# The first loads of a fused attention and MLP kernel: two queues for the first operand, a later table load on ScalarE, and four idle products on TensorE

## The chip, the cores and the metric

The kernel runs on one core of one Trainium2 chip. The metric is the device time of one execution in microseconds (us), lower is better. Three runs of the kernel before gave 574.39, 576.44 and 576.57 us, so the median is 576.44.

The engines are TensorE (PE, and PEld for its weight loads), VectorE (DVE), ScalarE (ACT), GpSimd (POOL) and SyncE (SP). SP and ACT each issue transfers on a queue of their own; the profile calls the issuing side SPq and ACTq. All the transfers of the page's "q1" are SP's, and those of "q10" are ACT's.

## The reference

```python
# q, k, v, f_logit: (4, 8, 768, 48) float32
f = 1.0 / (1.0 + np.exp(-f_logit))
for t in range(S):
    state = f[:, :, t, :, None] * state + np.einsum('bhd,bhe->bhde', k[:, :, t], v[:, :, t])
    y[:, :, t] = np.einsum('bhd,bhde->bhe', q[:, :, t], state)
# y as rows: (3072, 384)
h = x @ w_in                                   # (384, 2048)
g = h * (1.0 / (1.0 + np.exp(-1.702 * h)))
out = g @ w_out                                # (2048, 384)
```

## The kernel before

**Units.** The sequence is cut into 12 units of 256 tokens (three for each of four batches). For each unit `attention(n)` makes the gated linear attention in six levels (`level`), each a set of small products (`score`, tile `sc`), a scaling of X by the gates (`promote`, L561) and a masked copy into `A` (`evacuate`). The MLP of earlier units fills TensorE between those steps. Up to unit 3 the order on all engines is written out by hand (`opening`, then `PLAN`); PE and POOL keep the program's order throughout.

**The opening.** Unit 0 needs its three operands first. `load_raw(n, j, engines)` brings f_logit (j = 0), q (j = 1) or k (j = 2) into `raw`: one transfer for each of four pairs of heads, pair `a` going to the queue `engines[a * len(engines) // NP]`. With one engine in the list all four are on one queue. f and k are issued by SP, q by ACT (six transfers, because the first token is shifted). Eight semaphores serve the hardware transfers in turn, so a ninth transfer waits for the landing of the one that had its semaphore before. In the opening that means: k's third transfer waits for f's second, k's fourth for f's fourth, q's third for f's first, q's fourth for f's third, q's fifth and sixth for q's first and second, and the two transfers of the first weights (`fetch_weights`, L221) for k's first and second.

**The turns.** `turn` (L390 to L404) transposes `raw` through TensorE: two pieces of eight products for each operand into PSUM tiles `t` (L395; each product leaves two records, so a piece is 16 records), and ScalarE takes each piece out by two activations (L400): Sigmoid into `F` for f, Copy into `X` for k and q. The order is f (`begin_f`), k (`begin_k`, which then copies `Kc`, L536), q (`begin`). Only then come the first `sc` products of level 0.

**What stands before them.** DVE clears `ones` and then the whole of `A` (L135). ScalarE runs one Sigmoid on `ones` (L134), whose only use is to have the function table loaded; DVE then writes the ones again (L136). `keep_up(2, 192, ...)` makes two products of `A`'s cleared columns on TensorE, whose result nobody reads.

```python
def keep_up(times, columns=(NL - 1) * 64, of=None):
    if times:
        pt = bank([P, columns], f"idle_{next(serial)}")
    for _ in range(times):
        lhs, rhs = of or (ident, masks.rearrange("p l f t -> p (l f t)"))
        nc.tensor.matmul(pt, lhsT=lhs, rhs=rhs, start=True, stop=True)
```

Of the kernel before, what the change touches and what calls it, by code (L numbers as in the profile page):

```python
# [12 lines left out]
AF = mybir.ActivationFunctionType  # L13
# [10 lines left out]
def kernel(  # L24
# [33 lines left out]
    nc = tc.nc  # L58
# [3 lines left out]
    P = 128  # L62
# [51 lines left out]
    A = const.tile([P, 2 * NP, 2, HS], F32, name="A")  # L114
# [3 lines left out]
    def bank(shape, name, lane=None):  # L118

        if lane is None:  # L120
            lane = chosen.pop(0) if chosen else next(turns) % 4
        return ps.tile(shape, F32, tag=f"mm{lane}", name=name, bufs=1)
# [8 lines that stand above are left out]

    ones = const.tile([P, 1], F32, name="ones")
    nc.vector.memset(ones, 1.0)
    nc.scalar.activation(ones, ones, AF.Sigmoid)  # L134
    nc.vector.memset(A, 0.0)  # L135
    nc.vector.memset(ones, 1.0)  # L136
    serial = count()
    flat_A = A.rearrange("p c f t -> p (c f t)")
    keep_up(2, 192, (flat_A[:, :P], flat_A[:, :192]))

    R = U // 32
    RW = R * D + HS - D
# [49 lines left out]
    for r in range(NGR):  # L192
        ffs = range(r * FG, (r + 1) * FG)
        for ff in ffs[::2]:
            f = slice(ff * P, (ff + 2) * P)
# [13 lines left out]
    def fetch_weights(engine=nc.sync):  # L209
        n = state["fetch"]  # L210
        assert n < len(pairs) and n - PAIRS_AHEAD < state["done"] // 2
        state["fetch"] += 1
        dst, parts = pairs[n]
        if moe_w_in.dtype == F32:
            for part, src in parts:
                nc.sync.dma_start(out=part(dst), in_=src)
            return
        bits = wp.tile([P, 2 * DM * 2], I32, tag="bits", name=f"bits_{n}", bufs=PAIRS_AHEAD)
        by_dst = bits.rearrange("p (c f) -> p c f", c=dst.shape[1])
        for part, src in parts:  # L220
            engine.dma_start(out=part(by_dst), in_=src.bitcast(I32))  # L221
        fetched[n] = by_dst.rearrange("p c (f two) -> p c f two", two=2)

    def begin_pair(m):
        if m not in fetched:
            assert moe_w_in.dtype == F32
            todo.append(None)
            return
        dst, bits = pairs[m][0], fetched.pop(m)
        ve, lo, hi = nc.vector, bits[..., 0], bits[..., 1]  # L230

        def tmp(tag, bufs):
            t = wp.tile([P, 2 * DM], F32, tag=tag, name=f"{tag}_{m}", bufs=bufs)
            return t.rearrange("p (c f) -> p c f", c=dst.shape[1])

        t = {}

        def high():  # L240
            t["s"] = tmp("s", 1).bitcast(I32)
            ve.tensor_scalar(t["s"], hi, 3, None, op0=ALU.logical_shift_left)

        def low():
            t["r"] = tmp("a", 2).bitcast(I32)
            if m in R_BY_ACT:
                nc.scalar.activation(t["r"], lo.bitcast(U32), AF.Copy, scale=2.0 ** -29)
            else:
                ve.tensor_scalar(t["r"], lo.bitcast(U32), 2.0 ** -29, None, op0=ALU.mult)

        def both():
            ve.tensor_tensor(dst.bitcast(I32), t["s"], t["r"], ALU.add)
        nc.scalar.activation(hi.bitcast(F32), hi.bitcast(F32), AF.Prelu, scale=2.0 ** -112, alpha=-(2.0 ** 32))
        if m in R_BY_ACT:
            low()
        else:
            todo.append(low)
        todo.extend((high, both, None))
# [7 lines left out]
    def convert():  # L266

        if len(todo) <= NOP // 2:
            begin_next()
        if todo and todo[0]:  # L270
            todo.pop(0)()
        if todo and todo[0] is None:
            todo.pop(0)
            state["done"] += 2
# [10 lines left out]
    def load_raw(n, j, engines=(nc.sync,)):  # L285
        if n >= NALL:
            return
        b, s0 = n // NU, n % NU * U
        src = (f_logit, q, k)[j]
        first = s0 - (j == 1)  # L290

        def span(head, token, dims, d=0):
            return bass.AP(src.tensor, src.offset + ((b * H + head) * S + token) * D + d, dims)
        if n < N_FILL or (n == N_FILL and j in BY_PE):
            for a in range(NP):
                engine = engines[a * len(engines) // NP]
                to = by_pair[j][32 * a:32 * (a + 1), :, :R * D]
                if first < 0 and a == 0:

                    for r, rows in ((1, 16), (17, 15)):  # L300
                        engine.dma_start(
                            out=to[r:r + rows], in_=span(0, r * R - 1, [[R * D, rows], [S * D, 2], [1, R * D]])
                        )
                    engine.dma_start(out=to[:1, :, D:], in_=span(0, 0, [[R * D, 1], [S * D, 2], [1, (R - 1) * D]]))
                else:
                    engine.dma_start(out=to, in_=span(2 * a, first, [[R * D, 32], [S * D, 2], [1, R * D]]))
            return
        for f in (1, 0):
            for r in range(4):
                lo = 32 * (r % 2)  # L310
                width = R4 * D - lo
                part = span(r // 2, first + (0 if f else HALF), [[R4 * D, 32], [2 * S * D, NP], [1, width]], lo)
                nc.sync.dma_start(out=by_half[32 * r:32 * (r + 1), j, f, :, :width], in_=part)
            if f and first < 0:
                for r in range(4):
                    lo = 32 * (r % 2)
                    nc.sync.dma_start(
                        out=by_half[32 * r:32 * r + 1, j, f, :, :D - lo],
                        in_=q[b - 1, r // 2::2, S - 1:S, lo:].rearrange("a t d -> t a d"),
                    )  # L320
# [3 lines left out]
    def load_v(n):  # L324


        if n >= NALL:
            return
        b, s0 = n // NU, n % NU * U
        vts[n] = ld.tile([P, 2, DM], F32, tag="vt", name=f"vt_{n}", bufs=2)  # L330
        vrs[n] = ld.tile([P, DM], F32, tag="vr", name=f"vr_{n}", bufs=1)
        nc.sync.dma_start(
            out=vts[n][:, 1].rearrange("p (h d) -> p h d", h=H), in_=v[b, :, s0:s0 + HALF, :].rearrange("h p d -> p h d")
        )
        for i in range(4):
            t0 = s0 + U - 32 * (i + 1)
            nc.sync.dma_start(
                out=vrs[n][32 * i:32 * (i + 1)].rearrange("p (h d) -> p h d", h=H),
                in_=v[b, :, t0:t0 + 32, :].rearrange("h p d -> p h d"),
            )  # L340
# [1021 lines left out]
    def opening():  # L1362

        begin_f, begin, begin_k, begin_gates = units[0][0]
        next_f, next_q, next_k, next_gates = units[1][0]
        level, evacuate, turn_k = units[0][2]
        load_raw(0, 0)
        load_raw(0, 2)
        load_raw(0, 1, (nc.scalar,))
        fetch_weights()  # L1370
        begin_f()
        begin_gates()
        begin_k()
        begin()
        load_raw(1, 0)
        load_raw(1, 2)
        load_v(0)
        load_raw(1, 1)
        fetch_weights()
        fetch_weights()  # L1380
        for l in range(NL):
            chosen[:] = [2, 3][l % 2:][:1]
            level(l)
            if l in (2, 3):
                next_f((0, 4)[l - 2:][:1])
            elif l < NL - 1:
                keep_up(1)
            if l == 1:
                begin_pair(0)
                state["begin"] = 1  # L1390

        nc.scalar.activation(q_end, q_end, AF.Gelu_apprx_sigmoid)
        chosen[:] = [2, 3]
        turn_k(0)
        turn_k(2)
        for l in range(NL - 1):
            evacuate(l)
            if l == 1:
                units[0][3]()
        chosen[:] = [2, 3, 2, 3]  # L1400
        next_q()
        begin_pair(1)
        state["begin"] = 2
        evacuate(NL - 1)
        units[0][1][-2][1]()
        next_gates()
        for _ in range(NOP):
            convert()
        fetch_weights()

    fill = []
    opening()
    FIRST = 'k'
    PLAN = {
# [69 lines left out]
```

## Time and profile before

| | |
|---|---|
| median of three runs | 576.44 us (574.39 to 576.57) |
| the profiled execution | 574.38 us, of which the span is 572.6 |
| PE busy | 562.1 us (98% of the span) |
| DVE, ACT, POOL busy | 440.3, 291.7, 144.6 us |
| PE in the chain that ended last | 93% |
| first `t` product, first `sc` product | 4.63 us, 12.54 us |

The span runs from the first to the last instruction of the core; the 1.8 us beside it lie outside of it. The profile is of one execution, and its time is that of the quickest of the three runs. A busy PE is not a PE at its peak, and the shares of the whole span say little about the first 13 us, which are read here by themselves.

### The profile page before, as it was taken

The numbers are of one execution on the slowest core, as the hardware profiler recorded it, in microseconds if no ns is written. First come the engines' busy times: TensorE is split into PE (matmuls) and PEld (weight loads), VectorE is DVE, ScalarE is ACT, GpSimd is POOL, SyncE is SP. The second block draws the span as 40 slices with busy tenths as digits, with TensorE's granted clock in tenths as the row PEclk, the third lists the DMA queues.
The fourth block names the chain that finished last, engine by engine and source line by source line (L and its number), as shares of the span: only waits on it lengthen the run. The fifth ranks groups of instructions, "written<-read, shape, count | busy, mean of one in ns | idle before, by whom it ended". The sixth has DMA issues, their size and how long they took to land.

```text
span 572.6 us, 18599 instructions
## 1 busy us (share of the span) xinstructions
PE 562.1 (98%) x7870; PEld 515.3 (90%) x7870; DVE 440.3 (77%) x695; ACT 291.7 (51%) x592; POOL 144.6 (25%) x226
## 2 busy tenths in 40 slices
PE   7989999999999999999999999999999999999997
PEld 6767777686899999999999999999999999999996
DVE  2899688898997786887787888886888886462294
ACT  4755554332544573564564564564564573543440
POOL 4030320419451601501501501502501601303000
PEclk9999999999999999999999999999999999999999
DMA  7879695833262452363443344353361121001000
GB/s 194 194 181 230 152 254 135 238 81 87 72 177 58 125 134 57 99 158 79 114 123 68 99 118 104 108 129 69 98 158 44 50 55 30 30 2 29 29 1 28
DMA packets 85939, 60.01 MB, mean 105 GB/s; under 512 B 33441, under 2 KB 77633, under 8 KB 85857
## 3 DMA queue, kind: packets, MB, share of 16 engines
q1 hardware_dynamic: 85328, 58.21, 39.9%
q8 instruction: 62, 1.02, 0.8%
q10 hardware_dynamic: 529, 0.62, 0.4%
q14 instruction: 20, 0.16, 0.1%
HBM read 45.16 MB, written 8.91 MB: 94 GB/s over the span
## 4 chain that ended last, share of the span: by engine, by line
PE 93%; DVE 3%; DMA 1%; ACT 1%; issue 1%; SPq 0%; DVEq 0%
PE h L1080 28%; PE o_Y L938 14%; PE h L1174 10%; PE o_Z L938 9%; PE o L1188 7%; PE sc L467 6%; PE o_X L938 5%; PE o_W L938 4%; PE y L585 2%; PE y L743 2%; PE sc L696 2%; PE t L395 1%; DMA bits<-in_moe_w_in_dram 1%; DVE A L527 1%; DVE X L565 1%; DVE X L561 1%
## 5 line engine op out<-in xcount | busy, mean ns | idle before, releaser
L565 DVE TENSOR_TENSOR X<-X,tot 128x1024 f32<-128x1024 f32 x50 | 68.2, 1364 | 41.3 <-PE sc L467 37.0
L536 ACT COPY Kc<-X 128x512 f32<-128x512 f32 x72 | 48.4, 672 | 84.4 <-DVE X L565 71.2
L1080 PE MATMUL h<-E,w_in 128*128 128x128 f32 (+1 forms) x648 | 82.6, 276 | 0.0
L1080 PEld LDWEIGHTS h<-E,w_in 128*128 128x128 f32 x648 | 77.1, 192 | 0.5
L1108 DVE TENSOR_TENSOR g<-g,h 128x512 f32<-128x512 f32 (+1 forms) x92 | 55.4, 627 | 26.2 <-PE h L1080 18.9
L1038 POOL TENSOR_TENSOR E<-xT 128x128 f32<-128x128 f32 (+1 forms) x36 | 15.9, 453 | 231.3 <-DMA xT<-yT 231.3
L1174 PE MATMUL h<-xT,w_in 128*128 128x256 f32 x288 | 65.5, 382 | 0.0
L1174 PEld LDWEIGHTS h<-xT,w_in 128*128 128x128 f32 x288 | 53.9, 190 | 8.9 <-DMA xT<-yT 0.3
L1110 ACT ACTIVATE g<-g 128x512 f32<-128x512 f32 (+1 forms) x70 | 40.3, 588 | 34.9 <-DVE g L1108 34.8
L938 PE MATMUL o_Y<-T,S 128*128 128x192 f32 x320 | 57.6, 329 | 0.0
L938 PEld LDWEIGHTS o_Y<-T,S 128*128 128x128 f32 x320 | 52.3, 190 | 0.5
L1188 PE MATMUL o<-w_out,g 128*128 128x384 f32 x128 | 44.3, 492 | 0.0
L1099 ACT ACTIVATE g<-h 128x512 f32<-128x512 f32 (+1 forms) x70 | 37.0, 549 | 13.3 <-PE h L1080 11.4
L383 DVE STREAM_TRANSPOSE X<-raw 128x512 f32<-128x512 f32 x38 | 41.0, 1117 | 1.5 <-PE y L743 1.0
L527 DVE COPY_PREDICATED A<-masks,sc 128x256 f32<-128x256 uint32 (+1 forms) x98 | 42.0, 504 | 0.0
L758 ACT COPY yT<-y 48x256 f32<-48x256 f32 (+1 forms) x66 | 22.0, 369 | 30.1 <-PE y L743 29.6
L1080 PE MATMUL h<-E,N_c 128*128 128x128 f32 (+1 forms) x288 | 37.1, 275 | 0.0
L1188 PEld LDWEIGHTS o<-w_out,g 128*128 128x128 f32 x128 | 23.6, 190 | 14.6 <-issue 0.7
L1080 PEld LDWEIGHTS h<-E,N_c 128*128 128x128 f32 x288 | 35.1, 192 | 0.2 <-DVE osb L898 0.2
L467 PE MATMUL sc<-X,Kc 48*64 48x64 f32 x1344 | 28.2, 220 | 3.1 <-ACT Kc L536 1.4
L467 PEld LDWEIGHTS sc<-X,Kc 48*64 48x64 f32 x1344 | 24.0, 134 | 7.5 <-ACT Kc L536 3.6
L938 PE MATMUL o_X<-w_out,g 128*128 128x192 f32 x160 | 29.9, 332 | 0.3 <-ACT o_X L902 0.3
(131 smaller groups left out, 1088.2 us busy)
## 6 DMA issues: line engine op xcount, KB each, us to landing
bits<-in_moe_w_out_dram SPq DMA_DIRECT2D x8, 768.0 KB
raw<-in_f_logit_dram SPq DMA_DIRECT2D x48, 96.0 KB
raw<-in_k_dram SPq DMA_DIRECT2D x48, 96.0 KB
bits<-in_moe_w_in_dram SPq DMA_DIRECT2D x8, 576.0 KB
raw<-in_q_dram SPq DMA_DIRECT2D x44, 96.0 KB
k_tok<-z SPq DMA_DIRECT2D x64, 64.0 KB
kt<-k_tok SPq DMA_DIRECT2D x16, 256.0 KB
out_dram<-osb SPq DMA_DIRECT2D x20, 192.0 KB
```

The lines of the kernel that those rows point to most:

```text
L383: copied["turned"] = nc.vector.transpose(view(out, at, [[HALF, NP], [step, R4], [R4 * step, 32]]), by_half[:, j, f].rearrange("p a (j d) - ...
L467: nc.tensor.matmul(t["sc"][h][g * HS:(g + 1) * HS, a, s, :], lhsT=t["Kc", l][rows(h), x:x + HS], rhs=rhs(h, a, g), start=True, stop=True,)
L527: moved = nc.vector.copy_predicated(out=view(A, c * HALF + at, dims), mask=mask.bitcast(U32), data=got)
L536: nc.scalar.copy(c.rearrange("p (n two m) -> p n two m", two=2, m=m), view(X, KF * SLOT, [[2 * m, SLOT // (2 * m)], [(KR - KF) * SLOT + m, ...
L565: done = nc.vector.tensor_tensor(x, x, y, ALU.mult)
L938: nc.tensor.matmul(t[name], lhsT=lhs(f), rhs=rhs(f), start=(new and i == 0), stop=(i == HF - 1), skip_group_check=True,)
L1080: nc.tensor.matmul(ph[:, t], lhsT=WA[a][:, f // 2, f % 2 * P:(f % 2 + 1) * P], rhs=E[n][b], start=(root and t == 0), stop=not goes_on, ski ...
L1099: nc.scalar.activation(to, ph, AF.Copy, scale=float(sign))
L1108: copied["sum"] = nc.vector.tensor_tensor(to, to, part, ALU.add if sign > 0 else ALU.subtract)
L1110: nc.scalar.activation(to, to, AF.Gelu_apprx_sigmoid)
L1174: nc.tensor.matmul(ph, lhsT=w_in[:, ff // 2, c, ff % 2 * P:(ff % 2 + 1) * P], rhs=xTs[n][:, c, :], start=(c == 0), stop=(c == NK - 1))
L1188: nc.tensor.matmul(t["po"], lhsT=g[ff // FG][:, ff % FG, tt * P:(tt + 1) * P], rhs=w_out[:, ff, :], start=(ff == ffs[0]), stop=(ff == ffs[ ...
```

## The change

f's four transfers are split over SP and ACT, two on each. The Sigmoid that loads the table moves from the beginning of the program to behind ACT's eight transfers (two of f, six of q). The rewriting of `ones` moves from DVE to POOL. `A` is cleared in two pieces, the first of 192 columns, and `keep_up` makes four products of those 192 columns instead of two. The order of the instructions on each engine is otherwise that of before.

```diff
     ones = const.tile([P, 1], F32, name="ones")
     nc.vector.memset(ones, 1.0)
-    nc.scalar.activation(ones, ones, AF.Sigmoid)
-    nc.vector.memset(A, 0.0)
-    nc.vector.memset(ones, 1.0)
+    flat_A = A.rearrange("p c f t -> p (c f t)")
+    nc.vector.memset(flat_A[:, :192], 0.0)
+    nc.vector.memset(flat_A[:, 192:], 0.0)
     serial = count()
-    flat_A = A.rearrange("p c f t -> p (c f t)")
-    keep_up(2, 192, (flat_A[:, :P], flat_A[:, :192]))
+    keep_up(4, 192, (flat_A[:, :P], flat_A[:, :192]))
...
-        load_raw(0, 0)
+        load_raw(0, 0, (nc.sync, nc.scalar))
         load_raw(0, 2)
         load_raw(0, 1, (nc.scalar,))
+        nc.scalar.activation(ones, ones, AF.Sigmoid)
+        nc.gpsimd.memset(ones, 1.0)
         fetch_weights()
         begin_f()
         begin_gates()
```

## The prediction

> **What bounds the kernel now.** I read the page, then the waits of PE by stage, then the first 13 us: chain, timeline, windows. The page gives the shares of the chain that ended last:
>
> ```profile
> PE 93%; DVE 3%; DMA 1%; ACT 1%; issue 1%; SPq 0%; DVEq 0%
> ```
>
> PE's waits in the stretch from 60 to 160 us are 0.5 us in all, from 160 to 460 none are listed. All the change touches lies before 12.54 us, so the question is only how much sooner the first `sc` product starts, and whether that lead reaches the stretch in which PE never waits. The chain of the first 13 us:
>
> ```profile
> 0.74 0.40 SPq L306
> ...
> 2.12 2.38 DMA raw<-in_f_logit_dram
> 4.50 0.14 issue
> 4.63 5.18 PE t L395 x64
> 9.81 0.02 issue
> 9.84 0.67 ACT X L400 x2
> 10.50 0.02 issue
> 10.53 0.85 ACT Kc L536
> 11.38 1.11 ACT X L400 x4
> 12.49 0.04 issue
> ```
>
> f's last transfer is issued fourth on SP and lands at 4.50; then PE turns, then ScalarE. The timeline of ScalarE and its queue shows who else is near:
>
> ```profile
> 0.74 1.28 ACT L134 ACT_TABLE_LOAD   x1 [0.74 <-PEq L1468]
> 1.97 0.45 ACTq L301 DMA_DIRECT2D raw<-in_q_dram  x1
> 3.94 1.36 ACTq L306 DMA_DIRECT2D raw<-in_q_dram  x3
> 6.65 0.66 ACT L400 ACTIVATE F<-t 128x256 f32<-128x256 f32 x2 [4.41 <-DMA raw<-in_q_dram]
> 8.09 0.66 ACT L400 ACTIVATE F<-t 128x256 f32<-128x256 f32 x2 [0.78 <-PE t L395]
> 8.96 0.66 ACT L400 ACTIVATE X<-t 128x256 f32<-128x256 f32 x2 [0.21 <-PE t L395]
> 9.84 0.66 ACT L400 ACTIVATE X<-t 128x256 f32<-128x256 f32 x2 [0.21 <-PE t L395]
> ```
>
> ScalarE waits for PE 0.78 + 0.21 + 0.21 = 1.20 us between the first F and Kc: PE is late, by its own pace. The windows of L395 alone show why:
>
> ```profile
> 5.60:6.60 1.00, 1.00 (x13) 1.00 (x11) 1.00 1.07 299
> 6.60:7.60 1.00, 1.00 (x13) 1.00 (x11) 1.00 0.68 156
> 7.60:8.60 1.00, 1.00 (x22) 1.00 (x20) 1.00 0.92 317
> ```
>
> The first count is of records that touch the window: 13 in a us until 7.6, 22 behind it. The single records start in pairs 0.213 us apart before, 0.109 behind: the array runs at half pace up to 7.65 us, although the clock column reads 1.00 in all three rows (the trace's first clock record is a 1.0 at 7.65; nothing is recorded before). A piece of 16 records costs 1.71 us slow and 0.87 fast.
>
> **The change part by part.** All in the profiled execution's time (574.38 us, its span 572.6 and 1.8 around it).
>
> *A in two pieces, four idle products.* The clearing of A costs 0.91 us for 1024 columns, `ones` 0.06 for one; 192 columns lie near 0.06 + 0.16 = 0.22 us. It starts at 1.05 as before, so PE starts at 1.33 instead of 2.02. The four records of before start at 2.02, 2.50, 2.82 and 3.14; eight would start from 1.33 to 3.73 and leave PE free for the turns at 4.05. The other 832 columns end near 2.0 as now, and DVE's next job waits for POOL anyway (0.31 and 0.85 us idle). Cost of the split: nothing.
>
> *f on two queues.* The last of f's issues ends at 1.61 instead of 2.55. Landing: by issue time alone 4.50 - 0.94 = 3.56; if the bytes bound it, no sooner than 4.50. The four landed at 2.89, 3.38, 3.71 and 4.50 (the semaphores' counts in the trace), and 393 KB at the window's 235 GB/s (2.0 to 3.7 us) from the first packet at 1.8 is 3.5; I take 3.8. So the idle products, not f, set the start of the turns: 4.05 against 4.63, with 4.63 as the other end.
>
> *The half pace.* PE would be busy without a break from 1.33; now it stands still from 3.67 to 4.63. If the switch needs some 3 us of nearly full work (4.63 to 7.65 is 3.02), it comes between 4.3 and 7.65: each us sooner saves 0.49 us of the turns (1 - 0.109/0.213). The Trainium skill, "TensorE: Matmul & The Clock Gate", Part 1, says that the clock is released after a busy window of about 3.4 us and that this window runs freely, so the switch falls differently from run to run. This trace agrees in the 3.02 us of one execution; one trace cannot show the spread.
>
> *The table load.* This speaks against the change. ACT now issues two of f from 0.74, while q's first stays at 1.97 (it waits for POOL's clearing of raw, which ends at 1.94, not for the table). q's sixth waits for the landing of its second (4.97) and ends at 5.30. The load, 1.28, and the Sigmoid, 0.20, come behind that: the first F can start at 6.8, against 6.65 now. That PE has the piece earlier is of no use there. From then on, with PE ahead, ScalarE goes through without the 1.20 of waiting: four pairs at 0.69 (9.84 to 10.53), then 2.01 from Kc to `sc` (10.53 to 12.54) = 4.77, so `sc` starts at 11.57, 0.97 sooner. Bounds for the end of q's issues: 4.6 if its second lands with less beside it (F at 6.1, `sc` 1.67 sooner), or later (below). The skill's "ScalarE: Activation LUTs", What ACT_TABLE_LOAD costs, adds a drain of about 1.38 us to each switch. The row of the second load disagrees: Kc ends at 20.41, the load runs from 20.43 to 21.71 and its activation starts at 21.72. By that page `sc` would be at 12.95, 0.41 later than now.
>
> *k and q behind it.* Both are late already and only just hidden: k's fourth lands at 7.38 and is first read at 7.87; q's sixth lands at 9.17 and is read at 9.62. k's first still waits for POOL (1.97 against 2.59), its fourth for f's fourth (issued near 3.9 against 4.52): it lands near 6.8, no longer late. q's sixth is not sooner, and the first weights, which wait for k's first, start some 0.6 us earlier beside it. With q at 9.17, two pieces (1.76 and 0.2 to come out) end at 11.2, the last activations (0.6) at 11.85: `sc` at 11.9, 0.65 sooner. At 8.5 or less ScalarE decides (0.97); at 9.8 nothing is left. I take 0.75, from 0 to 1.67.
>
> *ones on POOL.* One small memset, 0.10 us by POOL's own, waiting for the Sigmoid (7.0). Behind it stands the first gate product, at 8.83 now, which needs all of F (near 8.2): hidden by a us; without that cover 0.1.
>
> *Behind 12.54.* Levels, conversions and later loads are released by these same engines. The second unit's f is turned at 16.45 and has landed at 13.57; the second weights' conversion at 25.24, landed at 22.99. These have 2 to 3 us to spare, so a lead of under 2 us passes through to PE's solid stretch and to the end.
>
> Sum: 574.38 - 0.75 = 573.6 for an execution like the profiled one. The median stands 2.06 above it. If those runs have the switch one window later (some 3.3 us), their turns cost 3.3 x 0.49 = 1.6 more, and the new kernel, with PE busy earlier, would mostly be spared it. I credit 0.65 of that 1.6: 576.44 - 0.75 - 0.65 = **575.0**, and 574.2 to 576.0 for this case alone.
>
> **The rivals.**
> 1. *q's last transfer takes it all.* The weights beside it push its landing to 9.8: 576.4. For: q's transfers need 2.4 to 3.9 us from issue to landing as weights join. Against: the dip of 156 GB/s from 6.6 to 7.6 leaves room.
> 2. *The clock decides.* The switch comes in all runs near 4.3, and the 2 us above the profiled run are the late switch: 574.38 - 1.2 = 573.2 as a median, 572.4 to 574.0. For: an idle gap of 0.96 us vanishes, and the three runs lie at two levels. Against: no run shows two switches, and ScalarE's F at 6.8 hides much of it.
> 3. *The table load takes the place of f's wait: slower.* ScalarE's chain needs 4.77 from the first F, so it loses from F at 7.77 on, which is q's issues ending at 6.27. If q's second needs as long as its sixth did (4.99 to 9.17, 4.18), it lands at 6.64, q's issues end at 6.96, F starts at 8.46, `sc` at 13.23: 0.69 late, 577.1. For: f's third and fourth now stand ahead of q on the queue. Against: f is 196 KB there and has landed by 3.8; q's second landed in 2.5 us beside the same bytes.
> 4. *The load costs more than its row.* Both loads of the trace let their activation follow within 0.02 us; the worst that a row bounds is a second load's time, 1.28 more: F at 8.1, `sc` at 12.87, 576.8. Against: both rows. The drain of the skill's page named above is a rule of this kind.
>
> That the change does not do what it says is excluded by the order of instructions: the ACT list has two f, six q, load, Sigmoid.
>
> **How the numbers follow.** Forecast 0.55; rival 1 0.12; rival 2 0.24; rival 3 0.06; rival 4 0.03. A measurement tells about 0.5% from no change, here 2.9 us, below 573.56 or above 579.3. Of rival 2 some 0.20 lies below 573.56, of the forecast 0.01; slower by so much needs F near 10.7 or a cause not seen here: 0.04. The range goes from rival 2's lower end to 576.9, two thirds of rival 3's price above the median: 572.4 to 576.9. It leaves out the costlier half of rival 3 and the tails of the others, under 2 in 10 together.
>
> **What would show it.** Idle records x8 from 1.33; `t` from 4.05; the load behind the last ACTq L306, F near 6.8; no wait for PE between the F and X pairs; `sc` near 11.8. Counts of 22 in L395's windows before 7.6 mean an earlier switch. Wrong: F after 7.8 (rival 3), PE waiting for q behind 9.2 (rival 1), or a lead at `sc` that is gone at 60 us.

## The result, and the profile after

The changed kernel has a median of 579.63 us (20 runs, 575.4 to 584.4) against 576.11 us of the kernel before on the same chip (20 runs, 574.4 to 577.4 but for a single one of 720.6): a ratio of 1.0053, 95% interval 1.0038 to 1.0068. The ratio leaves out the one execution in a slow state (584.4 us) and, like those below, is not the quotient of the two medians, which is 1.0061. The kernel is slower by half a percent; 575.0 us was predicted, with a range up to 576.9. The profiled execution took 575.4 us (span 573.7) and is one of the quickest: 6 of the 20 executions, with a mean granted clock of 0.999 or more, took 575.4 to 576.8 us, and the other 14, with 0.985 to 0.997, took 578.8 to 584.4. So two things have to be explained: about 1 us that the profiled executions show (575.40 against 574.38), and the rest of the 3.5 us between the medians, some 2.5 us, that they do not.

The page's line on the chain that ended last has 2% of DMA now, where there was 1%:

```profile
PE 92%; DMA 2%; DVE 2%; ACT 2%; issue 0%; ACTq 0%; POOL 0%; DVEq 0%; SPq 0%; POOLq 0%
```

The chain (start, duration, what) says which, as far as the turns of q:

```profile
2.38 3.53 DMA raw<-in_q_dram
5.90 0.02 issue
5.93 5.23 DMA raw<-in_q_dram
11.15 0.14 issue
11.29 1.98 PE t L394 x32
```

Before, the chain went from f's last transfer through 5.18 us of turns and through ScalarE. Now two transfers of q fill the time to 11.16: the second one (issued 2.38, landed 5.91), whose semaphore the sixth has to have, and the sixth itself, issued at 5.93 and landed at 11.16. Before, the sixth was issued at 4.99 and had landed at 9.17. f no longer stands in the chain. (Lines of the changed kernel have numbers one lower: L394 is L395 of before.)

The timeline of ScalarE, of SP and of PE shows the rest of the opening:

```profile
5.30 0.95 ACTq L305 DMA_DIRECT2D raw<-in_q_dram  x2
6.28 1.28 ACT L1369 ACT_TABLE_LOAD   x1 [6.28 <-DMA raw<-in_q_dram]
7.57 0.20 ACT L1369 ACTIVATE ones<-ones 128x1 f32<-128x1 f32 x1
7.68 0.64 ACT L399 ACTIVATE F<-t 128x256 f32<-128x256 f32 x2
8.51 0.66 ACT L399 ACTIVATE F<-t 128x256 f32<-128x256 f32 x2 [0.20 <-PE t L394]
```

```profile
5.53 0.87 SPq L220 DMA_DIRECT2D bits<-in_moe_w_in_dram  x2
```

SP's row of before, for comparison:

```profile
5.23 0.83 SPq L221 DMA_DIRECT2D bits<-in_moe_w_in_dram  x2
```

And PE, changed:

```profile
1.15 2.93 PE L130 MATMUL idle<-A 128*128 128x192 f32 x8 [1.15 <-DVE A L135]
4.79 6.24 PE L394 MATMUL t<-ident,raw 128*64 128x128 f32 x64 [0.71 <-DMA raw<-in_q_dram]
11.29 1.97 PE L394 MATMUL t<-ident,raw 128*64 128x128 f32 x32 [0.26 <-DMA raw<-in_q_dram]
14.00 0.70 PE L466 MATMUL sc<-X,Kc 48*64 48x64 f32 x32 [0.75 <-ACT X L399]
```

The eight records of the idle products end at 4.08, and the turns start at 4.79, not sooner than the 4.63 of before: the last of f's transfers lands at 4.55 from two queues, where it landed at 4.50 from one. SP's first weights, 768 KB in two transfers, start at 5.53 and so stand 0.40 us *ahead* of q's sixth; before they started at 5.23, 0.24 *behind* it. The first `sc` comes at 14.00 against 12.54. Of that 1.46 us, about 1.0 is left from 100 us on (each ScalarE instruction laid beside the same one of before), and 573.7 - 572.6 = 1.1 at the end.

The windows of L394 alone show the pace of the array (the first count is of records that touch the window; 22 in a us is full pace):

```profile
6.60:7.60 1.00, 1.00 (x13) 1.00 (x11) 1.00 0.60 110
7.60:8.60 1.00, 1.00 (x13) 1.00 (x12) 1.00 1.07 352
8.60:9.60 1.00, 1.00 (x14) 1.00 (x12) 1.00 1.06 249
9.60:10.60 1.00, 1.00 (x18) 1.00 (x16) 1.00 1.05 235
```

With four idle products in front the array stayed at half pace until 10.01 us, later than with two (7.65).

### The profile page after: what moved, and what is told of

Read it like the earlier page. It is cut to its first block, busy times and chain, and to the rows that moved or that the text cites. A ratio compares the mean times of both kernels' runs of the same rounds, so it can differ in the third digit from the quotient of the medians.

```text
span 573.7 us, 18608 instructions
## 1 busy us (share of the span) xinstructions
PE 564.4 (98%) x7874; PEld 517.5 (90%) x7874; DVE 439.3 (77%) x695; ACT 291.7 (51%) x592; POOL 145.3 (25%) x227
## 4 chain that ended last, share of the span: by engine, by line
PE 92%; DMA 2%; DVE 2%; ACT 2%; issue 0%; ACTq 0%; POOL 0%; DVEq 0%; SPq 0%; POOLq 0%
PE h L1079 28%; PE o_Y L937 14%; PE h L1173 10%; PE o_Z L937 9%; PE o L1187 7%; PE sc L466 6%; PE o_X L937 5%; PE o_W L937 4%; PE y L742 2%; PE y L584 2%; PE sc L695 2%; DMA raw<-in_q_dram 2%; DMA bits<-in_moe_w_in_dram 1%; DVE A L526 1%; PE t L394 1%; DVE X L564 1%
## 5 line engine op out<-in xcount | busy, mean ns | idle before, releaser
L1037 POOL TENSOR_TENSOR E<-xT 128x128 f32<-128x128 f32 (+1 forms) x36 | 17.1, 485 | 231.1 <-DMA xT<-yT 231.1
L409 POOL TENSOR_SCALAR F<-F 128x1024 f32<-128x1024 f32 x10 | 13.0, 1300 | 70.5 <-ACT F L412 70.5
L1177 ACT ACTIVATE g<-h 128x256 f32<-128x256 f32 x48 | 17.8, 382 | 24.7 <-PE h L1173 24.5
```

## The experiments

All ratios are to the kernel before on the same chip, with their 95% intervals. Times are of the profiled execution of each, in us. "q's sixth" is issued, landed, as the semaphores' counts in the trace have it; "weights" is the issue of the first of the first weights' two transfers; "switch" is when the array comes to full pace.

| run | first F | q's sixth | weights | first sc | switch | median us | ratio |
|---|---|---|---|---|---|---|---|
| before | 6.65 | 4.99, 9.17 | 5.23 | 12.54 | 7.65 | 576.11 | |
| changed | 7.68 | 5.93, 11.16 | 5.53 | 14.00 | 10.01 | 579.63 | 1.0053 [1.0038, 1.0068] |
| r1 changed again | 7.62 | 5.87, 10.70 | 5.60 | 13.55 | 6.42 | 579.06 | 1.0053 [1.0030, 1.0076] |
| r2 idle products only | 6.45 | 4.88, 7.87 | 5.31 | 12.41 | 6.04 | 576.02 | 1.0006 [0.9993, 1.0018] |
| r3 two queues only | 6.51 | 5.97, 12.46 | 5.37 | 15.30 | 9.93 | 578.31 | 1.0043 [1.0020, 1.0066] |
| r4 later table only | 6.93 | 5.17, 8.66 | 5.37 | 12.75 | 8.17 | 575.27 | 0.9992 [0.9980, 1.0003] |
| r5 changed, f on one queue | 6.89 | 5.14, 9.07 | 5.29 | 12.17 | 5.81 | 575.40 | 1.0000 [0.9988, 1.0012] |
| r6 changed, q's sixth on SP | 7.16 | 5.64, 7.97 | 6.17 | 11.50 | 4.16 | 575.30 | 0.9991 [0.9978, 1.0003] |
| r7 changed, more idle products | 7.74 | 5.93, 11.05 | 5.57 | 13.96 | 7.08 | 577.69 | 1.0047 [1.0022, 1.0072] |
| r8 idle products, q's sixth on SP | 6.93 | 5.27, 8.11 | 5.63 | 13.51 | 9.35 | 575.70 | 1.0002 [0.9991, 1.0013] |
| r9 before, q's sixth behind weights | 6.64 | 6.18, 12.51 | 5.32 | 15.36 | 10.30 | 579.52 | 1.0054 [1.0034, 1.0073] |
| r10 two queues, table first, q's sixth on SP | 5.63 | 5.46, 7.67 | 6.05 | 11.46 | 5.03 | 575.87 | 0.9998 [0.9982, 1.0015] |

**The parts one by one.** r1 is the changed kernel unaltered.

> The changed kernel once more, for the clock of its single executions. Two theories. Transfers: q's sixth transfer lands at 11.16 us instead of 9.17, the first sc product starts at 14.00 instead of 12.54, and this lead lost is all there is: every execution some 1 to 1.5 us longer (577 to 578), at a granted clock of 1.000. Clock: most executions lose one to five stretches of some 3.4 us at half clock (a mean of 0.997 for one, 0.994 for two), each worth about 1.7 us: median 579 to 580, and the executions at 1.000 lie near 576. If the profile falls on one of these, its clock rows show where.

It repeats the ratio, and 8 of its 12 executions have a mean granted clock below 0.998. r2 keeps the idle products and the split of `A`, with the table first and f on one queue:

```diff
 # before, with
-    nc.vector.memset(A, 0.0)
+    nc.vector.memset(flat_A[:, :192], 0.0)
+    nc.vector.memset(flat_A[:, 192:], 0.0)
...
-    keep_up(2, 192, (flat_A[:, :P], flat_A[:, :192]))
+    keep_up(4, 192, (flat_A[:, :P], flat_A[:, :192]))
```

> Only A in two pieces and four idle products instead of two; the table load first and f on SP alone as before. Transfers theory: q lands as before (9.2), PE is not sooner than f (4.6), so 575.5 to 576.2 and clock 1.000. Clock theory, by the idle products (PE released early, then too little work): means under 1.000 in most executions and a median of 578 to 580, as with the whole change.

r3 takes the two queues alone, r4 the later load alone:

```diff
 # r3: before, with
-        load_raw(0, 0)
+        load_raw(0, 0, (nc.sync, nc.scalar))
 # r4: before, with
-    nc.scalar.activation(ones, ones, AF.Sigmoid)
     nc.vector.memset(A, 0.0)
-    nc.vector.memset(ones, 1.0)
...
         load_raw(0, 1, (nc.scalar,))
+        nc.scalar.activation(ones, ones, AF.Sigmoid)
+        nc.gpsimd.memset(ones, 1.0)
```

> Only f on two queues; two idle products and the table load first as before. Transfers theory: q's second lands later, its sixth is issued behind the first weights and lands after 10.5, sc after 13.3: 576.8 to 577.8, clock 1.000. Clock theory, by the idle products: like before, 576.1. Clock theory, by PE standing still for q: means under 1.000 here too, median above 578.

> Only the table load behind q's transfers (and ones on POOL); f on SP alone, two idle products. Both theories: q's issues end at 5.3 as before, the first F starts at 6.8 instead of 6.65, sc at 12.6 to 12.7: 576.0 to 576.4 with a clock of 1.000. A drain or any hidden cost of the late load would show as F after 7.3.

r2 and r4 do nothing that can be measured; r3 carries the loss, 1.0043. Its q's sixth is issued behind both weights (5.37 and 5.73 against 5.97) and PE waits for it:

```profile
12.59 1.97 PE L395 MATMUL t<-ident,raw 128*64 128x128 f32 x32 [1.75 <-DMA raw<-in_q_dram]
```

r5 puts f back on one queue in the changed kernel and leaves the rest:

```diff
 # changed, with
-        load_raw(0, 0, (nc.sync, nc.scalar))
+        load_raw(0, 0)
```

> The changed kernel with f on SP alone again; the late table load and the four idle products stay. If the two queues are the cause: q's sixth lands near 9 as before, sc starts at 12.5 to 12.8, 575.3 to 576.3, and the granted clock is 0.999 or more in nearly all executions. If the late table load or the idle products were needed for the loss as well: 577 or more.

The loss is gone (1.0000). So the loss needs the two queues; the table and the idle products do not make it by themselves.

**Two queues, or the order behind them?** r6 leaves f on two queues and gives only q's sixth to SP, ahead of the weights:

```diff
 # changed, with
-        load_raw(0, 1, (nc.scalar,))
+        load_raw(0, 1, (nc.scalar, nc.scalar, nc.scalar, nc.sync))
```

> The changed kernel, f on two queues, with one transfer moved: q's sixth goes out on SP, where it stands ahead of the first weights. Theory that the weights overtake it: it lands by 9 instead of 11.16, PE does not wait for q, sc starts at 12.0 to 12.8, 575 to 576, the clock near 1.000. Rival, that two queues slow every landing (bytes shared with k and f): q's sixth lands after 10 here too, and the time stays above 577.5.

It lands at 7.97 though issued only 0.29 sooner, `sc` comes at 11.50 and the loss is gone (0.9991). r7 asks instead whether the pace of the array is to blame, by three idle products between the turns of k and of q:

```diff
 # changed, with
         begin_k()
+        chosen[:] = [1]
+        keep_up(3)
         begin()
```

> The changed kernel with three more idle products (320 columns, 1.6 us at full clock) between k's turns and q's, where PE now stands still for q. Theory that the clock falls back because PE has too little work there: the executions under 0.998 go from about 7 in 10 to a few, the median falls to 577 to 578, while sc stays at 13.5 to 14.2 in an execution at full clock. Rival, that the clock falls for another reason (later in the levels, or by the idle products in front): the share under 0.998 stays, and the median stays at 579 or above.

q lands as late as ever (11.05) and `sc` comes at 13.96. The outcome is mixed: the median falls to 577.69 and 5 of 12 executions are below 0.998, nearer to the first theory than to its rival, but the ratio of 1.0047 [1.0022, 1.0072] cannot be told from that of the change. Filling the wait does not undo the loss; whether it lessens it stays open. r8 joins r2 and the order of r6, r10 the two queues, the idle products and that order, with the table first as in the kernel before:

```diff
 # r8: r2, with; r10: changed, with the Sigmoid and the second memset of ones where they were before, and
-        load_raw(0, 1, (nc.scalar,))
+        load_raw(0, 1, (nc.scalar, nc.scalar, nc.scalar, nc.sync))
```

> The kernel before with the four idle products and with q's sixth transfer on SP ahead of the first weights; f on SP alone, table load first. If q's landing is what bounds the turns once the clock is released early, sc starts at 12.0 to 12.3 and the median is 574.6 to 575.3, a little under before. If k's landing (7.4 to 7.6) bounds: sc near 12.4, 575.3 to 575.8, no difference that shows.

> A version meant to beat both: f on two queues, four idle products, q's sixth on SP ahead of the first weights, and the table load first again. With q landing by 8 and F no longer behind the table (5.8 to 6.6 instead of 7.16), PE's own turns and k's landing (6.7) set the pace: sc at 11.2 to 11.6 where the clock is released early, median 574.6 to 575.4, at most 0.2% under before. If F was not what bounded: as with the late table load, 575.3.

Neither differs from the kernel before (1.0002, 0.9998), though r10 was meant to beat it and had `sc` 1.08 us sooner; where most of that lead goes, near 28 us, is seen below. r8's `sc` at 13.51 is an execution with a late switch (9.35), with q there at 8.11. r9 is the cleanest test: the kernel before, with f on one queue and the table first, and q's sixth on SP just behind the first weights.

```diff
 # before, with
-        load_raw(0, 1, (nc.scalar,))
         fetch_weights()
+        load_raw(0, 1, (nc.scalar, nc.scalar, nc.scalar, nc.sync))
```

> The kernel before (f on SP alone, table load first, two idle products) with one thing done alone: q's sixth transfer goes out on SP behind the two transfers of the first weights. If that order is the cause by itself: it lands at 11.5 or later, sc starts at 14.3 to 15.5, the median is 2 to 4 us over before (578 to 580), and a quarter or more of the executions have a clock under 0.998. If the loss needs f on two queues: no more than 0.5 us over before.

It has a loss as large as the change's, 1.0054, from the order alone. The order is a harsher one, behind both transfers of the weights, and `sc` is late by 2.82 us where the change had 1.46:

```profile
5.32 0.82 SPq L221 DMA_DIRECT2D bits<-in_moe_w_in_dram  x2
6.18 0.47 SPq L306 DMA_DIRECT2D raw<-in_q_dram  x1
```

```profile
12.64 1.97 PE L395 MATMUL t<-ident,raw 128*64 128x128 f32 x32 [1.54 <-DMA raw<-in_q_dram]
```

Issued 1.19 later than before, q's sixth lands 3.34 later. Sorted by its place against the first weights, the landings of q's sixth line up over all 20 profiled executions: issued 0.36 to 0.59 ahead (r2, r6, r8, r10, s4, t2) it lands at 7.66 to 8.11, 0.15 to 0.26 ahead (before, r4, r5, s2, s3) at 8.34 to 9.22, 0.23 to 0.59 behind the first transfer (changed, r1, r7, r11, r12, s1, t1) at 10.70 to 11.89, and behind both (r3, r9) at 12.46 and 12.51.

**The other 2.5 us.** An execution of 575.4 does not explain a median of 579.63. All 14 slower executions have a mean granted clock of 0.997 or less. A stretch of 3.41 us at half pace costs 1.7 us, 0.003 of 577. By this estimate they had one such stretch (0.997, three of them) to five (0.985), and the middle one of all 20, at 0.994, had two: some 3.4 us. The profiles below bear the estimate out: r11 has one stretch and 0.997, s1 two and 0.994, t1 three and 0.991. Two more single profiled executions of the changed kernel, the second with two idle products instead of four, were meant to catch a slower one.

> The changed kernel, one more profile, to see an execution whose clock falls back. Theory: the clock goes to half after a stretch of some 3.4 us in which PE stood still for q (8 to 11 us), and stays there through the levels, whose products are few (14 to 28 us), so the sc rows cost about twice as much there. Rival: it falls in the solid part behind 60 us.

> The changed kernel with two idle products instead of four (A still cleared in two pieces), one profile: as the one before, 577 to 583; with a fall of the clock its place is seen, and without one sc starts at 13.5 to 15.

They took 578.3 and 578.1 us. In both the distance to the kernel before grows a second time, at 25 to 27 us, at the turn of the second unit's q; in r11 that, and not the wait for q, is where the clock falls. The row of that turn before:

```profile
22.68 1.97 PE L395 MATMUL t<-ident,raw 128*64 128x128 f32 x32 [0.24 <-ACT kn L649]
```

The timeline of PE and the windows of r11:

```profile
22.71 1.09 PE L647 MATMUL tkn<-ident,X 128*128 128x128 f32 x8
25.55 3.59 PE L394 MATMUL t<-ident,raw 128*64 128x128 f32 x32 [1.75 <-issue]
29.06 1.15 PE L695 MATMUL pd<-vt,kn 64*64 64x48 f32 x64
```

```profile
24.00:26.00 2.00, 0.46 (x5) 0.49 (x7) 2.00 (x8) 0.47 (x1) 0.00 (x0) 0.87 0.87 250
26.00:28.00 2.00, 2.00 (x23) 2.00 (x22) 1.84 (x6) 0.44 (x2) 0.00 (x0) 0.50 0.35 66
28.00:30.00 2.00, 2.00 (x76) 1.76 (x72) 0.00 (x0) 1.04 (x4) 0.00 (x0) 0.77 0.32 51
```

PE stands still for 1.75 us with nothing that the profile names ("issue"), then the granted clock (the third column from the end) is 0.50 from 25.49 for 3.41 us, and 32 turns take 3.59 us instead of 1.97. The changed kernel's own profile has neither. r1, r3, r9 and r12 have the standstill (1.75, 1.63, 1.63, 1.90), r9 the clock too.

What PE waits for is not named, but can be inferred from the instruction queue, q8 on the page: 62 packets of 16 KB. In every execution with such a standstill, PE goes on 1.4 to 1.6 us after the end of one of these packets (r11: 22.73 + 1.27 = 24.00, PE at 25.55). Where PE does not stand still there, that packet (the queue's second) starts 1.9 to 4.2 us ahead of `tkn`, the turn of the first unit's k just before (before: 18.96 and 21.35). Where it does, the packet starts up to 1.1 us behind `tkn`, and in the five executions of this kind so far (r1, r3, r9, r11, r12) 3.6 to 5.4 us after SP issued the third weights (the first `w_out`, 768 KB). My reading was that PE, late by q, asks for its next block when those 768 KB are already queued. Four kernels were to try it. s1, s2 and s4 move the `fetch_weights()` of `w_out` behind the first loop over `evacuate`, in the changed kernel, the kernel before and r6; s3 goes the other way.

> The changed kernel, with the third pair of weights (the first w_out, 768 KB) issued on SP behind the second unit's v instead of ahead of it, some 8 us later. Theory (code behind weights): TensorE's second block of instructions, 16 KB on the instruction queue, is read at 18.2 to 19.7 us in the executions without a stall near 25 us and at 22.4 to 25.1 in those with one (r1, r3, r9, r11, r12), 3.6 to 5.4 us after w_out was issued: TensorE, late by q, asks for it when the 768 KB are already queued. With w_out gone from there the block is read before 20.5 us, the stall of 1.6 to 1.9 us [<-issue] is gone, fewer than a quarter of the executions show a granted clock below 0.998 (14 of 20 and 8 of 12 before), and the ratio to the kernel before is 1.000 to 1.003: q's own lateness of 1.0 to 1.5 us stays. Rival (lateness alone): the stall and the clock come from q's lateness whatever is queued; stall stays, ratio 1.004 to 1.006.

> The kernel before, with the same move of the first w_out. Theory (code behind weights): the second block was in time already, so nothing large goes; executions below 0.998 (13 of 86 until now) become rarer, ratio 0.997 to 1.000. Rival (w_out itself is then late for its conversion near 36 us, or stands in front of another block): a wait near 31 to 37 us, ratio 1.001 to 1.003.

> The changed kernel with q's sixth transfer on SP ahead of the weights (r6) and w_out late as above. r6 had its first sc at 11.50 us against 12.54, and lost the gain at a stall of 1.31 us [<-issue] at 27.9, where the third block of instructions was read at 25.34, no sooner than in the kernel before (25.39). Theory (code behind weights): the third block too had waited for w_out; now it is read before 24.8, the stall at 27 to 28 us is under 0.5, and the ratio is 0.996 to 0.999. Rival: the third block is asked for at a point of its own, the stall stays over 1 us, ratio 0.999 to 1.001 as in r6.

```diff
 # changed (s1), before (s2), r6 (s4), with
         load_raw(1, 1)
         fetch_weights()
-        fetch_weights()
...
         for l in range(NL - 1):
             evacuate(l)
             if l == 1:
                 units[0][3]()
+        fetch_weights()
```

The move of these three did nothing: v's transfers are written further down still, so `w_out` kept its place on SP (issued at 19.34 in s1, 0.11 sooner than in the changed kernel, and still ahead of v's next transfer). They count as repeats of the change (1.0061 [1.0035, 1.0087]), of the kernel before (1.0002 [0.9990, 1.0015]) and of r6 (0.9987 [0.9972, 1.0002]). s3 did move it, 2.1 us sooner, in a kernel whose q is not behind the weights:

```diff
 # before, with
-        load_v(0)
         load_raw(1, 1)
         fetch_weights()
         fetch_weights()
+        load_v(0)
```

> The kernel before, with the first unit's v issued behind the second and third pairs of weights, so that w_out is issued 2.5 us sooner, near 16.2 us, while q and the rest of the opening stay as they were. Theory (code behind weights): the second block of instructions is now asked for behind w_out although nothing is late; it is read 3 us or more after w_out's issue, TensorE stands 1 to 2 us [<-issue] between 22 and 27 us, and the ratio is 1.001 to 1.005. Rival (lateness alone): no such stall, ratio 0.999 to 1.001, unless v itself comes late, which a wait on vr or vt would show.

```profile
23.91 0.43 PE L395 MATMUL t<-ident,raw 128*64 128x128 f32 x3 [0.24 <-ACT kn L649]
25.96 2.33 PE L395 MATMUL t<-ident,raw 128*64 128x128 f32 x29 [1.62 <-issue]
```

The same standstill, in the middle of 32 turns whose operand is there, and a ratio of 1.0048 [1.0031, 1.0066] (median 578.46). The block is read at 23.40, 6.7 us after `w_out`'s issue. The first unit's v is late here too, but only DVE waits for it (1.59 us), not PE. So one transfer order is enough for the standstill. t1 and t2 then take `w_out` away for certain, behind the second unit's v, in the changed kernel and in r6:

```diff
 # changed (t1) and r6 (t2), with
         load_raw(1, 1)
         fetch_weights()
-        fetch_weights()
...
         evacuate(NL - 1)
         units[0][1][-2][1]()
+        fetch_weights()
```

> The changed kernel with the first w_out really behind the second unit's v on SP: in s1 it had kept its place (issued at 19.34 us), since v's transfers are written further down, so s1 repeats the change. Here w_out is issued at 27 to 31 us. Theory (code behind weights): TensorE's second block of instructions is read before 21.5 us instead of 22.4 to 25.4, or lags only behind the 768 KB of w_in that are still ahead of it; TensorE's stall [<-issue] near 25 to 28 us (1.62 to 2.18 us in r1, r3, r9, r11, r12, s1, s3) is under 0.6 us; fewer than a third of the executions are below 0.998 of the granted clock; ratio 1.001 to 1.0035, q's own lateness. Rival (the block waits for the 768 KB of w_in that stand directly in front of w_out, or for something else): the stall stays over 1.2 us, ratio 1.004 to 1.006. A block that is read later than w_out's new issue, or a wait for w_out near 36 us, would add a loss of its own and would show at 31 to 38 us.

> The changed kernel with q's sixth transfer on SP ahead of the weights (r6, and s4, whose w_out had kept its place), and the first w_out behind the second unit's v as in t1. r6 and s4 had sc at 11.50 and 11.31 us against 12.54 and stood still for 1.31 and 1.95 us [<-issue] at 28, their third block of instructions being read at 25.3 and 25.7. Theory (code behind weights): the third block too had waited for w_out; it is now read before 24.8, the stall near 28 us is under 0.6, ratio 0.996 to 0.9985. Rival (the third block is asked for at a point of its own): stall over 1.2 us, ratio 0.998 to 1.000.

t2 came out as its theory had it: the third block is read at 22.63 instead of 25.3 to 25.7, the standstill of r5, r6, r10 and s4 near 28 us (1.31 to 1.95 us) is gone, the median is 574.79 us and the ratio 0.9983 [0.9970, 0.9996]. Of the 17 ratios here it is the only one whose interval lies below 1, by a sixth of a percent, from 7 executions; it is not told apart from 0.9987 of s4 and 0.9991 of r6. t1 did not: its profile has no standstill near 25 us, yet the ratio stays 1.0053 [1.0041, 1.0065], and all six executions have a granted clock below 0.998. The block was read at 24.00, with PE itself late (`tkn` at 27.14). Its timeline and windows show another place for the same loss:

```profile
12.02 2.44 PE L394 MATMUL t<-ident,raw 128*64 128x128 f32 x32 [2.87 <-DMA raw<-in_f_logit_dram]
```

```profile
10.00:12.00 2.00, 0.00 (x0) 0.01 (x1) 0.83 (x1) 0.72 (x1) 1.76 (x4) 1.00 1.07 194
12.00:14.00 2.00, 1.99 (x31) 2.00 (x32) 0.00 (x0) 0.66 (x2) 0.26 (x2) 0.84 0.96 225
14.00:16.00 2.00, 1.25 (x33) 0.85 (x33) 0.00 (x0) 1.22 (x3) 0.00 (x0) 0.50 0.74 151
```

The array had its full pace at 6.53, did k's turns by 9.15, and stood for 2.87 us until q's sixth landed at 11.88 (the profile names the second unit's f, which landed at the same time; PE goes on 0.14 after q's sixth here, and 0.13 after it in the changed kernel). The clock fell at 13.36 and stayed at half for 10.24 us, three times 3.41. In s1 the same wait was 3.45 us and the clock was at half from 11.32 for 3.41, and again from 28.39, after a standstill of 2.18.

**What stays open.** A late q costs twice: itself, and a wait of PE that can let the clock fall, be it the wait for q or the later one for code. How the 14 slower executions divide over these two was not seen, since none of them was profiled. With q late, 35 of 48 executions with four idle products (changed, r1, s1, t1) are below 0.998, and 7 of 17 with two (r3, r9): an early switch, with PE then waiting the longer for q, may let the clock fall more often, but no run changes this alone. That the block of code waits *behind* the 768 KB, and is not merely asked for late, is argued from the times of its packets: s3 and t2 agree with it, t1 neither shows nor refutes it, and no trace has the moment of asking. Nor does one tell `w_out` from the weights issued just ahead of it: in t1, without `w_out` there, the block was read at 24.00, while those landed (23.39 and 24.11).

## Why the prediction was wrong, point by point

- **The split of A and the idle products: right.** PE starts at 1.15 (1.33 was worked out), the last record ends at 4.08 (4.05). Alone they cost nothing that can be measured, and brought nothing (r2: 1.0006).
- **f on two queues: too much credited.** Of 3.56 to 4.50 I took 3.8; the last of f landed at 4.55. The profiled execution is at the late end, though: over the 12 with two queues it landed at 3.87 to 4.55 (median 4.24), over the 8 with one at 4.42 to 4.79 (median 4.54), and the first turn started 0.13 to 0.25 us later (median 4.48 against 4.67). Of the 0.94 us saved in issue, some 0.3 reach the landing. The Trainium skill, "DMA: Bandwidth & Descriptors", Issuing engines are not separate DMA queues, says that transfers started by several engines run on the same DMA engines and that only the time to issue them is saved. The 4.55 agrees (the issue ended 0.9 us sooner, the landing did not move); the other runs agree in part, with the 0.3.
- **The half pace: the mechanism stands, the credit does not.** In all the profiled executions the switch comes at 7.65 to 10.30 us with two idle products (7 of them, median 9.44) and at 3.99 to 10.01 with four (13, median 6.04). So the longer stretch of work does tend to bring the switch forward, as rival 2 supposed, but with a spread of 6 us and not to 4.3 in all runs. It is worth little all the same: in r2, with the switch at 6.04, PE has done f's turns by 7.29 and waits 0.40 for k, and `sc` comes 0.13 sooner than before. Where the switch is early in the changed kernel (s1 at 4.50, t1 at 6.53) PE only waits the longer for q. The 0.65 us that I credited were not there.
- **The table load: the price right, the start wrong.** 1.28 us and an activation 0.01 behind (6.28, 7.57), no drain: rival 4 is refuted here. Alone it moved F to 6.93 and `sc` by 0.21 (r4). In the changed kernel F came at 7.68, since q's issues end at 6.25 and not at 5.30. The step "q's sixth waits for the landing of its second (4.97)" used the landing of before: behind two transfers of f on its own queue the second lands at 5.91. Rival 3 named exactly this ("f's third and fourth now stand ahead of q on the queue") and I argued it away with f landed by 3.8. What rival 3 made of it is not what cost the time: by its own sum ScalarE loses only from F at 7.77 on.
- **"q's sixth is not sooner": the step that failed.** I bounded its landing by 8.5 and 9.8, with the weights starting some 0.6 us earlier "beside it". It was issued 0.94 later, and k's first landed at 5.51 (5.21 before), so the weights started 0.30 later, yet in front of it: it landed at 11.16 here, and at 10.70 to 12.51 in the other runs with this order. The way from there to `sc` was right (2.73 us in the sum, 2.84 measured); the landing alone turned the 0.65 to 0.97 us gained into 1.46 lost. Rival 1 had this wait of PE, but stopped at a landing of 9.8. r9 shows that the order alone can make such a ratio, r5 and r6 that without it the rest of the change is worth nothing that can be measured.
- **"Slower by so much needs ... a cause not seen here".** There was one: the sum had no term for what a lateness does afterwards. A wait of PE of about half of 3.41 us can cost another 1.7 us (3.41 us at half pace) and more where the half pace lasts longer, and PE's own code, by the inference above, came late. The sentence "a lead of under 2 us passes through to PE's solid stretch" was taken to hold for a loss as well; it does in the profiled execution (1.46 at `sc`, 1.1 at the end) and not in r11 (1.37 at `sc`, 3.9 at the end). Nor had the second weights 2 to 3 us to spare: by the same counts they had landed whole at 24.33, not 22.99, 0.9 us ahead of their conversion at 25.24.

## What to carry to other kernels

When a transfer is moved to a second queue, list what stands behind it there, which semaphore each of those waits for, and which large transfer of the other queue now gets in front: here 0.6 us in the order of issue were worth 2 us in the landing, and 0.9 us saved in issue landed the first operand some 0.3 us sooner. Keep the last small operand of the opening ahead of the first large prefetch; that was worth more than everything that the change did. And price a loss in front of a busy array apart from a gain: a wait can bring the clock down, and 1.4 us at the first `sc` cost 3.9 us at the end of r11.

## What was not expected of the hardware

- **Code can come late, as far as the packets tell.** PE stood for 1.3 to 2.2 us with nothing named ("issue") and went on 1.4 to 1.6 us after the end of a 16 KB packet on the instruction queue, in eleven profiled executions (r1, r3, r5, r6, r9 to r12, s1, s3, s4). The Trainium skill, "Runtime: NRT & Kernel Launch", Instruction fetch mechanics, says that code is refilled in blocks of 16 KB while the engine executes, and that the cost of crossing a block is mostly hidden. The size agrees; if the inference holds, next to 1.5 MB of weights (two times 768 KB) the cost was not hidden.
- **The clock can fall after a window that is only half idle.** The lengths in the clock's rows (3.41, 6.83, 10.24, 13.65, 17.07 and 23.89 us) are one to seven times 3.41 us, so windows of that length can be counted back from each fall, or on from the switch. The clock fell to half for 3.41 us (10.24 in t1) after windows in which PE had stood for 1.67 (r9), 1.70 (r11), 1.86 (s3), 1.95 (s4), 2.07 (t1), 2.18 and 2.81 us (s1), all its waits over 0.15 us added. It stayed up after 1.75 (r3), 1.72 (r1) and 1.54 us (r9). So over these runs it fell from 1.86 us on, never up to 1.54, and went either way near half a window. The Trainium skill, "TensorE: Matmul & The Clock Gate", Part 1, gives the free-running window of about 3.4 us, which agrees, but lets the clock go down after an idle window; here one with PE idle for about half of it did.
- **The first half pace does not show in the clock column.** The rows from 6.60 to 9.60 above read 1.00 at 13 or 14 records per us, against 22 at full pace; a later fall does show, as 0.50 in r11 and t1.
